# A fused attention, gated MLP and rotation kernel: batch 1's loads issued one by one, each behind a decoded tile of w_in

## The chip, the core and the metric

The program runs on one core of one Trainium2 chip. The metric is the device time in microseconds of one execution. A core has five instruction streams: PE (matmul), DVE (VectorE), ACT (ScalarE), POOL (GpSimd) and SP (SyncE, used here only to issue transfers). Each works through its own instructions in the order in which the program wrote them and waits on semaphores for the others.

## The reference

Three stages, on 4 batches of 768 tokens and 384 channels (8 heads of 48):

```python
# 1. gated linear attention, per batch and head
for t in range(S):
    state = f[:, :, t, :, None] * state + k_t (outer) v_t      # f = sigmoid(f_logit)
    y[:, :, t] = q_t @ state
# 2. gated MLP with a mixing over tokens
h = gelu_tanh(x @ w_in);  u, v = halves of h                    # w_in 384 x 1024
v_n = (v - mean(v)) / sqrt(var(v) + 1e-6) * g_ln
v_s = einsum('ts,bsd->btd', w_sg, v_n) + b_sg[None, :, None]    # w_sg 768 x 768
x = x + (u * v_s) @ w_out
# 3. rotation and a second mixing over tokens
theta = x @ w_theta
y = w_tok_r @ (x * cos(theta)) + w_tok_i @ (x * sin(theta))
u = x + y;  out = u + relu(u @ w_ch)
```

The weights arrive as 64-bit floats and are turned into 32-bit ones on the chip ("decoded").

## The kernel before

**Matmuls in three passes.** Every 32-bit operand of stages 2 and 3 is split into a high and a low part (`ACT` writes the high part, `DVE` subtracts and writes the low one), and a product is three matmuls (L782 to L784).

**Decoding.** A weight tile is loaded as raw 64-bit words into a buffer `st` (or `raw`), then one ACT instruction (L431) and four DVE instructions (L432 to L435) build the 32-bit value in `dt`, and L445 (ACT) and L446 (DVE) write its two parts to their place. `w_in` is cut into 12 tiles of 128x256, in the program's order (column block 2, k 0 to 2), (block 3, k 0 to 2), then blocks 0 and 1. Blocks 2 and 3 give v (one matmul group of 512 columns for each 128 tokens), blocks 0 and 1 give u. "Background" tiles (w_theta, w_ch and the two big mixing weights) go through the two `raw` buffers and are stored decoded to device memory for later.

**Attention.** A batch is done in two halves of 384 tokens, a half in four units of two heads. A half loads `f` (one tile, a single buffer `f` for all halves but one) and four `qkv` tiles. For batches 1 to 3 the loads are issued on POOL, for batch 0 on SP. Then, for batches 1 to 3: ACT computes the sigmoid by Tanh and Copy (L568, L569), DVE scans it (L572, L577), ACT takes Ln and Exp (L582, L583), and each unit has four products on DVE (L611 to L614), transposes (L627), state updates and scores on PE (L639, L648), a masked copy on DVE (L660), a chain of five or six small DVE steps that carry the state (L676, L680, L685, function `state`), and two more groups of matmuls (L703, L721).

**Order.** The body records operations in a `Plan`, each with an engine, a duration written by hand and a due time `vt`. A list scheduler then fixes the order of every engine's instructions, from these durations alone. `Buf` objects carry the dependencies that the scheduler sees. The semaphores that the chip waits for are put in afterwards, from the memory that the instructions really touch; an order that the scheduler chose between a POOL and an SP instruction that share no memory is therefore not enforced on the chip, while two instructions on one engine keep theirs. While PE has nothing to do in the first 100 us of the plan, the scheduler fills in matmuls of an identity (L1031), whose results nobody reads.

**The gate.** All loads of batches 1 to 3 come, in the plan, behind one POOL instruction, a copy of one element of the last decoded tile of `w_in` (L1041, k 2 of block 1) into the tile `gate`; the object that stands for it is called `first`, and the loads name it as a dependency (`later`).

Of the kernel before, what the change touches and what calls it, by code (L numbers as in the profile page):

```python
# [8 lines left out]
F32 = mybir.dt.float32  # L9
F32R = mybir.dt.float32r  # L10
I32 = mybir.dt.int32
# [6 lines left out]
P = 128  # L18
# [5 lines left out]
NK = DM // P  # L24
# [5 lines left out]
QKV = 2 * TH + NC2 * 2 * D + HP - D  # L30
WC = 256
# [28 lines left out]
HF0, HF1, V_AT, U_AT, DENSE = (-60.0, -40.0), (-25.0, -10.0), -35.0, -27.0, -33.0  # L60
# [262 lines left out]
def body(tc, ctx, att, qkv, flog, w_in, g_ln, w_sgT, b_sg, w_out, w_theta, w_rT, w_iT, w_ch, out):  # L323
    nc = tc.nc
# [19 lines left out]
        nc.vector.memset(t, value)  # L344
        return t

    gate = const.tile([P, 1], F32, name="gate")
    halfpi = fill("halfpi", math.pi / 2)
    mhalf = fill("mhalf", -0.5, NS)
    bends = const.tile([P, B, 2, NP, NC2], F32, name="bends")  # L350
# [15 lines left out]
    def make_state(attention):  # L366
# [21 lines left out]
        g.scr2 = [Buf(t=scratch2) for _ in range(2)]  # L388
        return g

    def nothing():
        pass

# [5 lines left out]
    def dma(pl, eng, nbytes, fn, r=(), w=(), wp=(), vt=None):  # L399
        pl.op(eng, {"SP": 0.47, "ACT": 0.66, "POOL": 1.05}[eng], fn, r, w, wp, dma=nbytes, vt=vt)  # L400
# [10 lines left out]
    def load_f32(pl, g, d, src, vt, background=False):  # L411

        n = src.shape[-1]
        get = lambda: d.t[:, :n]
        if src.dtype != I64:
            dma(pl, "SP", n * 512, lambda: nc.sync.dma_start(get(), src), w=[d], vt=vt - 3)
            return
        raw = pl.buf(g.raw if background else g.st, [P, 2 * TH], I32)
        dma(pl, "SP", n * 1024, lambda: nc.sync.dma_start(raw.t[:, : 2 * n], src.bitcast(I32)), [], [raw], vt=vt - 3)

        def bits():
            r = raw.t[:, : 2 * n].rearrange("p (n two) -> p n two", two=2)
            return r[:, :, 0], r[:, :, 1]

        def op(dur, fn, eng="DVE"):
            pl.op(eng, dur, fn, [raw], [d], vt=vt)

        V, iget = nc.vector, lambda: get().bitcast(I32)


        op(a1(n), lambda: nc.scalar.activation(get(), bits()[1].bitcast(F32), AF.Abs), "ACT")  # L431
        op(v2(n), lambda: V.tensor_scalar(get(), get(), TINY, None, ALU.max))  # L432
        op(v2(n), lambda: V.tensor_scalar(iget(), iget(), 3, 0x3FFFFFFF, ALU.logical_shift_left, ALU.bitwise_and))
        op(v1(n), lambda: V.scalar_tensor_tensor(iget(), bits()[1], -0x40000000, iget(), ALU.bitwise_and, ALU.bitwise_or))  # L434
        op(v1(n), lambda: V.scalar_tensor_tensor(iget(), bits()[0], 29, iget(), ALU.logical_shift_right, ALU.bitwise_or))  # L435
# [75 lines left out]
                half(pl, g, b, hf, x, carry, v0 + hf * (NP + 1) * step, step)  # L511
        return xst

    first = Buf()

    def half(pl, g, b, hf, xst, carry, vt, step):
        A = nc.scalar.activation
        eng = "SP" if b == 0 else "POOL"
# [10 lines left out]
            tiles = [(t, t) for t in (pl.buf(g.qkv, [P, QKV]) for _ in range(NP))]  # L529
        groups = (GROUPS0, GROUPS1)[hf] if b == 0 else [(0, NP)]  # L530
        qk, parts = [], []
        later = [first] if b else []
        for p, (t, root) in enumerate(tiles):
            for p0, p1 in groups:
                if p0 == p:
                    dma(
                        pl, eng, P * (p1 - p0) * TH * 4,
                        lambda gp=slice(p0, p1): q[eng].dma_start(f.t[:, gp], flog[b, hf][:, gp]), later, wp=fp[p0:p1],
                    )
            part = [Buf(of=root) for _ in range(3)]  # L540
            dma(pl, eng, P * QKV * 4, lambda t=t, p=p: q[eng].dma_start(t.t, qkv[b, p, hf]), later, wp=part)
            qk.append(t)
            parts.append(part)
        pl.vt = vt
# [43 lines left out]
    def unit(pl, g, b, hf, p, f, fb, seed, sb, be, bb, t, parts, xst, carry):  # L588
# [84 lines left out]
        def state(c):  # L673
            (s0, b0), (s1, b1) = S[c], S[c + 1]
            if hf == 0 and c == 0:
                pl.op("DVE", 0.117, lambda: V.tensor_copy(s1(), U(0)), r=[ps], w=[b1])  # L676
            elif c % 2 or c == 0:
                b1 = fulls[c // 2] if c % 2 else b1
                s1 = (lambda: st.t[:, 2 * NC2 + c // 2]) if c % 2 else s1
                pl.op("DVE", 0.117, lambda: V.tensor_add(s1(), s0(), U(c)), r=[ps, b0], w=[b1])  # L680
            else:
                be_ = be[:, c // 2 - 1 : c // 2]
                pl.op(
                    "DVE", 0.117,
                    lambda: V.scalar_tensor_tensor(s1(), st.t[:, 2 * NC2 + c // 2 - 1], be_, U(c), ALU.mult, ALU.add), r=[ps, fulls[c // 2 - 1], bb], w=[b1],  # L685
                )
            if c % 2:
                s2, b2 = S[c + 1]
                pl.op(
                    "ACT", 0.23, lambda: nc.scalar.activation(s2(), s1(), AF.Copy, scale=be[:, c // 2 : c // 2 + 1]), r=[bb, fulls[c // 2]], w=[b2]  # L690
                )
# [342 lines left out]
    with tc.manual_schedule():  # L1034
        def between():

            weights_in(pl, g, (2, 3), V_AT)
            weights_in(pl, g, (0, 1), U_AT)
            last = g.win[NK - 1][1]
            pl.op(  # L1040
                "POOL", 0.1, lambda: nc.gpsimd.tensor_copy(gate, win[:, 1, NK - 1, 2 * WC - 1 : 2 * WC].bitcast(F32)), [last], [first],  # L1041
                vt=U_AT,
            )
            pl.vt = U_AT
            dma(pl, "SP", 2048, lambda: nc.sync.dma_start(gcol, g_ln), wp=[g.const])
            dma(pl, "SP", P * 3072, lambda: nc.sync.dma_start(bbc, b_sg.partition_broadcast(P)), wp=[g.const])

        x = attention(pl, g, 0, *HF0, (*HF1, between))
        pl.vt = DENSE
# [187 lines left out]
```

## Time and profile before

| | |
|---|---|
| median of 3 runs | 677.27 us (672.85 to 678.81) |
| the profiled execution | 677.74 us, of which the trace spans 676.0 us |
| PE busy | 616.3 us, 91% of the span |
| DVE busy | 453.6 us, 67% |
| ACT busy | 342.3 us, 51% |
| POOL busy | 99.5 us, 15% |
| mean granted TensorE clock | 0.975 |

A busy share is an average over stages. The first 60 us belong to batch 0's attention and the decoding, with few real matmuls; then, to about 350 us, the first part of stage 2 and the attention of batches 1 to 3 run side by side with the background decoding; the last half is almost only matmuls. Granted clock is the clock that PE was given, as a share of 2.4 GHz: 1.00 is 2.4, 0.50 is 1.2 GHz.

### The profile page before, as it was taken

The page shows a single profiled execution, that of the slowest core. Times are in us where ns is not written, and L with a number is a line of the kernel's source. Part 1 is how long each engine was busy: PE and PEld are TensorE (multiplying, and loading weights), DVE is VectorE, ACT ScalarE, POOL GpSimd, SP SyncE. Part 2 cuts the span into 40 slices and gives each one's busy share as a digit, 9 for nine tenths or more (in the row PEclk, how much of TensorE's full clock was granted, in tenths as well). Part 3 has the DMA queues.
Part 4 walks back from the last instruction along what each step waited for, and adds up shares of the span by engine and source line. Part 5 has one row for each costly group of instructions (what it writes and reads, how often), then busy time and mean ns, then how long its engine had stood idle before and what let it go on. Part 6 is the DMA issues. An engine that isn't in the chain of part 4 may idle for free.

```text
span 676.0 us, 15027 instructions
## 1 busy us (share of the span) xinstructions
PE 616.3 (91%) x5953; PEld 569.8 (84%) x5953; DVE 453.6 (67%) x1077; ACT 342.3 (51%) x728; POOL 99.5 (15%) x178
## 2 busy tenths in 40 slices
PE   8788688989999988988989999899999999999996
PEld 8667567778788876878878999799989998998995
DVE  6999778969999897889979333741482175148203
ACT  6658587646685665675536421740291055019200
POOL 2000222143241340341131100000000000000000
PEclk9899969999999998999999999999999999999998
DMA  9522836377578787477575455058628844860762
GB/s 331 190 84 74 285 120 217 120 264 270 170 252 248 245 258 270 147 245 250 173 264 212 144 190 182 23 165 253 207 77 277 252 154 156 252 219 25 250 194 76
DMA packets 49296, 131.50 MB, mean 195 GB/s; under 512 B 6816, under 2 KB 17248, under 8 KB 48960
## 3 DMA queue, kind: packets, MB, share of 16 engines
q1 hardware_dynamic: 38656, 88.95, 41.2%
q0 software_dynamic: 10560, 41.49, 17.7%
q8 instruction: 49, 0.80, 0.5%
q14 instruction: 31, 0.25, 0.1%
HBM read 100.93 MB, written 24.77 MB: 186 GB/s over the span
## 4 chain that ended last, share of the span: by engine, by line
PE 42%; DVE 23%; ACT 11%; DMA 11%; issue 9%; POOL 2%; SPq 0%; DVEq 0%; POOLq 0%; ACTq 0%
PE mm L782 14%; PE mm L783 13%; PE mm L784 13%; DMA f<-in_flog 3%; DMA scratch<-wt 3%; DMA dt<-in_w_sgT 2%; DMA raw<-in_w_iT 2%; DVE s L680 2%; DVE dt L434 1%; DVE dt L435 1%; ACT ar L791 1%; DVE s L685 1%; DVE am L660 1%; POOL xst L755 1%; DVE tmp L845 1%
## 5 line engine op out<-in xcount | busy, mean ns | idle before, releaser
L782 PE MATMUL mm<-st,ar 128*128 128x384 f32 x480 | 164.9, 344 | 2.5 <-DMA st<-scratch 2.4
L783 PE MATMUL mm<-st,ar 128*128 128x384 f32 x480 | 161.4, 336 | 0.0
L784 PE MATMUL mm<-st,ar 128*128 128x384 f32 x480 | 161.4, 336 | 0.0
L801 ACT CAST x<-xst 128x384 fp32r<-128x384 f32 x72 | 36.9, 513 | 146.8 <-DVE xst L806 126.7
L806 DVE TENSOR_TENSOR xst<-xst,mm 128x384 f32<-128x384 f32 x48 | 25.7, 552 | 115.4 <-PE mm L784 115.4
L782 PEld LDWEIGHTS mm<-st,ar 128*128 128x128 f32 x480 | 90.9, 189 | 5.1 <-DMA st<-scratch 2.7
L783 PEld LDWEIGHTS mm<-st,ar 128*128 128x128 f32 x480 | 91.0, 190 | 0.1
L784 PEld LDWEIGHTS mm<-st,ar 128*128 128x128 f32 x480 | 90.8, 189 | 0.0
L782 PE MATMUL mm<-win,x 128*128 128x512 f32 (+1 forms) x144 | 56.6, 393 | 7.4 <-DVE tmp L845 3.7
L782 PE MATMUL mm<-x,win 128*128 128x384 f32 x168 | 58.4, 348 | 0.0
L784 PE MATMUL mm<-win,x 128*128 128x512 f32 (+1 forms) x144 | 54.1, 376 | 3.0 <-DVE x L802 3.0
L791 ACT CAST ar<-tmp 128x384 fp32r<-128x384 f32 x80 | 37.7, 509 | 37.7 <-DVE tmp L850 36.8
L784 PE MATMUL mm<-x,win 128*128 128x384 f32 x168 | 56.3, 335 | 0.0
L783 PE MATMUL mm<-x,win 128*128 128x384 f32 x168 | 56.2, 335 | 0.0
L783 PE MATMUL mm<-win,x 128*128 128x512 f32 (+1 forms) x144 | 53.5, 372 | 0.1
L802 DVE TENSOR_TENSOR x<-xst,x 128x384 fp32r<-128x384 f32 x72 | 37.8, 553 | 7.7 <-ACT x L801 6.4
L792 DVE TENSOR_TENSOR ar<-tmp,ar 128x384 fp32r<-128x384 f32 x80 | 41.0, 553 | 0.7 <-ACT ar L791 0.2
L782 PE MATMUL mm<-ar,wout 128*128 128x384 f32 x96 | 35.6, 371 | 4.2 <-DVE tmp L845 2.4
L782 PEld LDWEIGHTS mm<-win,x 128*128 128x128 f32 x144 | 27.8, 193 | 13.1 <-DVE tmp L845 5.4
L784 PE MATMUL mm<-ar,wout 128*128 128x384 f32 x96 | 33.3, 347 | 1.1 <-DVE wout L446 1.1
L755 POOL DMA_DIRECT2D xst<-y x60 | 30.7, 516 | 20.8 <-ACT y L732 10.9
L783 PE MATMUL mm<-ar,wout 128*128 128x384 f32 x96 | 33.4, 348 | 0.4 <-DVE ar L792 0.4
(146 smaller groups left out, 1227.2 us busy)
## 6 DMA issues: line engine op xcount, KB each, us to landing
st<-scratch SPq DMA_DIRECT2D x132, 384.0 KB, 3.8
qkv<-in_qkv POOLq DMA_DIRECT2D x24, 536.0 KB, 6.1
scratch<-wt POOLq DMA_DIRECT2D x24, 384.0 KB, 4.1
raw<-in_w_rT SPq DMA_DIRECT2D x12, 384.0 KB, 5.7
raw<-in_w_iT SPq DMA_DIRECT2D x12, 384.0 KB, 3.9
f<-in_flog POOLq DMA_DIRECT2D x6, 768.0 KB, 4.8
scratch<-st POOLq DMA_DIRECT2D x12, 384.0 KB, 6.7
out<-xst SPq DMA_DIRECT2D x24, 192.0 KB, 2.0
```

What stands on the lines that cost most here:

```text
L434: op(v1(n), lambda: V.scalar_tensor_tensor(iget(), bits()[1], -0x40000000, iget(), ALU.bitwise_and, ALU.bitwise_or))
L435: op(v1(n), lambda: V.scalar_tensor_tensor(iget(), bits()[0], 29, iget(), ALU.logical_shift_right, ALU.bitwise_or))
L680: pl.op("DVE", 0.117, lambda: V.tensor_add(s1(), s0(), U(c)), r=[ps, b0], w=[b1])
L755: lambda r0=r0, n=n, kc=kc, o=64 * j + off: q[yq].dma_start(xst.t[r0 : r0 + n, kc], y.t[o : o + n].rearrange("p i a t -> p (i a t)")),
L782: nc.tensor.matmul(o, h0, h1, start=start, stop=False)
L783: nc.tensor.matmul(o, h0, l1, start=False, stop=False)
L784: nc.tensor.matmul(o, l0, h1, start=False, stop=stop)
L791: pl.op("ACT", a1(n), lambda: nc.scalar.copy(tiles()[0], src.t[:, :n]), [src], [hi])
L792: pl.op("DVE", v1(n), lambda: V.tensor_sub(tiles()[1], src.t[:, :n], tiles()[0].bitcast(F32)), [src, hi], [lo])
L801: pl.op("ACT", a1(TH), lambda: nc.scalar.copy(X[hf][:, 0, k], T()), [src], [hi])
L802: pl.op("DVE", v1(TH), lambda: V.tensor_sub(X[hf][:, 1, k], T(), X[hf][:, 0, k].bitcast(F32)), [src, hi], [lo])
L806: pl.op("DVE", v1(TH), lambda: V.tensor_add(T(), T(), ps.t[:, :TH]), [ps], [xst[hf].parts[k]])
```

## The change

`gate` gets six columns and `first` becomes a list of six objects, `loaded`, one for each of the first six decoded tiles of `w_in` (blocks 2 and 3). For each of them POOL copies one element into its column. Only the loads of batch 1's first half name these: `f` the first tile, `qkv` 0 to 3 the second to the fifth. The loads of `g_ln` and `b_sg` name the first, and all background loads name the sixth. Batches 2 and 3 and the second half of batch 1 name none; their buffers hold them back. In `state` the three durations that the scheduler reckons with, 0.117 us each, become 0.2, 0.16 and 0.19.

```diff
-    gate = const.tile([P, 1], F32, name="gate")
+    gate = const.tile([P, 2 * NK], F32, name="gate")
+    loaded = [Buf() for _ in range(2 * NK)]
...
-        dma(pl, "SP", n * 1024, lambda: nc.sync.dma_start(raw.t[:, : 2 * n], src.bitcast(I32)), [], [raw], vt=vt - 3)
+        dma(pl, "SP", n * 1024, lambda: nc.sync.dma_start(raw.t[:, : 2 * n], src.bitcast(I32)), [loaded[-1]] if background else [], [raw], vt=vt - 3)
...
-    first = Buf()
...
-        later = [first] if b else []
+        gate_ = lambda i: [loaded[i]] if b == 1 and hf == 0 else []
...
-                        lambda gp=slice(p0, p1): q[eng].dma_start(f.t[:, gp], flog[b, hf][:, gp]), later, wp=fp[p0:p1],
+                        lambda gp=slice(p0, p1): q[eng].dma_start(f.t[:, gp], flog[b, hf][:, gp]), gate_(0), wp=fp[p0:p1],
...
-            dma(pl, eng, P * QKV * 4, lambda t=t, p=p: q[eng].dma_start(t.t, qkv[b, p, hf]), later, wp=part)
+            dma(pl, eng, P * QKV * 4, lambda t=t, p=p: q[eng].dma_start(t.t, qkv[b, p, hf]), gate_(p + 1), wp=part)
...
-                pl.op("DVE", 0.117, lambda: V.tensor_copy(s1(), U(0)), r=[ps], w=[b1])
+                pl.op("DVE", 0.2, lambda: V.tensor_copy(s1(), U(0)), r=[ps], w=[b1])
...
-                pl.op("DVE", 0.117, lambda: V.tensor_add(s1(), s0(), U(c)), r=[ps, b0], w=[b1])
+                pl.op("DVE", 0.16, lambda: V.tensor_add(s1(), s0(), U(c)), r=[ps, b0], w=[b1])
...
-                    "DVE", 0.117,
+                    "DVE", 0.19,
...
-            last = g.win[NK - 1][1]
-            pl.op(
-                "POOL", 0.1, lambda: nc.gpsimd.tensor_copy(gate, win[:, 1, NK - 1, 2 * WC - 1 : 2 * WC].bitcast(F32)), [last], [first],
-                vt=U_AT,
-            )
             pl.vt = U_AT
-            dma(pl, "SP", 2048, lambda: nc.sync.dma_start(gcol, g_ln), wp=[g.const])
-            dma(pl, "SP", P * 3072, lambda: nc.sync.dma_start(bbc, b_sg.partition_broadcast(P)), wp=[g.const])
+            for i, on in enumerate(loaded):
+                t, c, k = (gate[:, i : i + 1], *divmod(i, NK))
+                src = win[:, 1, k, (c + 2) * WC : (c + 2) * WC + 1].bitcast(F32)
+                pl.op("POOL", 0.1, lambda t=t, src=src: nc.gpsimd.tensor_copy(t, src), [g.win[k][c + 2]], [on], vt=U_AT)
+            dma(pl, "SP", 2048, lambda: nc.sync.dma_start(gcol, g_ln), [loaded[0]], wp=[g.const])
+            dma(pl, "SP", P * 3072, lambda: nc.sync.dma_start(bbc, b_sg.partition_broadcast(P)), [loaded[0]], wp=[g.const])
```

After the change every line number from about L395 on is 1 to 3 higher. Since a list scheduler sets the order, every engine's order changes from the first microseconds on. Two places matter most.

POOL, from the second seed fill of batch 0 (`ar2`) on, before. `f0`, `qkv0` to `qkv3` are batch 1's first half, `gate` the gate, `stat0` the statistics of v:

```order
L551 MEMSET ar2_0_114 128x384 x4
L567 MEMSET seed0_415 128x1536
L981 TENSOR_TENSOR stat0_865<-stat0_865,mhalf_81 128x3
L1041 COPY gate_78<-win_87 128x1
L538 DMA f0_1089<-in_flog 128x1536
L541 DMA qkv0_1102<-in_qkv 128x1072
L541 DMA qkv1_1116<-in_qkv 128x1072
L541 DMA qkv2_1130<-in_qkv 128x1072
L541 DMA qkv3_1143<-in_qkv 128x1072
L490 DMA scratch1_91<-st2_1091 128x768
```

The same place of POOL, after:

```order
L553 MEMSET ar2_0_115 128x384 x4
L569 MEMSET seed0_409 128x1536
L1045 COPY gate_78<-win_87 128x1
L540 DMA f0_523<-in_flog 128x1536
L1045 COPY gate_78<-win_87 128x1 x2
L543 DMA qkv0_842<-in_qkv 128x1072
L1045 COPY gate_78<-win_87 128x1
L543 DMA qkv1_860<-in_qkv 128x1072
L1045 COPY gate_78<-win_87 128x1
L543 DMA qkv2_882<-in_qkv 128x1072
L1045 COPY gate_78<-win_87 128x1
L543 DMA qkv3_900<-in_qkv 128x1072
```

The five loads moved from behind the first statistics of v to ahead of them, each behind its copy, in POOL's own order.

DVE, from the split of the last tiles of `w_in` (`st2` to `st4` are the first tiles of w_sg) to batch 1's first scan (L577 on `f0`), before:

```order
L446 TENSOR_TENSOR win_87<-dt2_1048,win_87 128x256
L993 SCALAR_TENSOR_TENSOR ar0_0_997<-tmp1_895,stat0_865,ar0_0_997 128x512
L993 SCALAR_TENSOR_TENSOR ar0_0_997<-tmp2_911,stat0_865,ar0_0_997 128x512
L742 TENSOR_TENSOR y1_1038<-y1_1038,at1_100 48x3x64 x2
L802 TENSOR_TENSOR x1_90<-xst1_0_726,x1_90 128x384
L446 TENSOR_TENSOR st2_1091<-dt0_1054,st2_1091 128x384
L446 TENSOR_TENSOR st3_1097<-dt1_1061,st3_1097 128x384
L446 TENSOR_TENSOR st4_1122<-dt2_1087,st4_1122 128x384
L572 TENSOR_SCALAR seed0_415<-f0_1089 128x12
L577 SCALAR_TENSOR_TENSOR f0_1089<-f0_1089,seed0_415 128x1536
L614 TENSOR_TENSOR qkv0_1102<-qkv0_1102,f0_1089 128x384
L802 TENSOR_TENSOR x1_90<-xst1_0_726,x1_90 128x384
```

DVE around the same scan (now L579) after the change:

```order
L437 SCALAR_TENSOR_TENSOR dt0_519<-st3_182,dt0_519 128x256
L601 TENSOR_TENSOR ar2_0_115<-ar2_0_115 128x384
L436 TENSOR_SCALAR dt1_367<-dt1_367 128x256
L436 TENSOR_SCALAR dt2_373<-dt2_373 128x256
L574 TENSOR_SCALAR seed0_409<-f0_523 128x12
L437 SCALAR_TENSOR_TENSOR dt1_367<-st1_173,dt1_367 128x256
L437 SCALAR_TENSOR_TENSOR dt2_373<-st2_178,dt2_373 128x256
L438 SCALAR_TENSOR_TENSOR dt0_519<-st3_182,dt0_519 128x256
L579 SCALAR_TENSOR_TENSOR f0_523<-f0_523,seed0_409 128x1536
L603 SCALAR_TENSOR_TENSOR ar1_0_146<-ar2_0_115,ar1_0_146 128x384
L438 SCALAR_TENSOR_TENSOR dt1_367<-st1_173,dt1_367 128x256
L438 SCALAR_TENSOR_TENSOR dt2_373<-st2_178,dt2_373 128x256
```

The scan moved from behind all 12 tiles of `w_in` and three tiles of w_sg into the decoding of the first five tiles, among the last products of batch 0's attention.

## Rows read from the trace of the kernel before

**Rows 1.** Busy time by stretch: PE, PEld, DVE, ACT, POOL, granted clock, DMA share, GB/s

```profile
204.00:250.00 46.00, 43.40 (x600) 39.97 (x601) 43.43 (x102) 30.42 (x57) 15.20 (x27) 1.00 0.76 242
450.00:500.00 50.00, 49.56 (x290) 48.81 (x289) 19.55 (x40) 15.16 (x32) 0.00 (x0) 1.00 0.71 221
```

**Rows 2.** The same view in stretches of 4 us

```profile
76.00:80.00 4.00, 1.21 (x8) 0.89 (x6) 0.96 (x2) 3.45 (x3) 0.00 (x0) 1.00 1.04 382
80.00:84.00 4.00, 0.95 (x3) 0.52 (x4) 3.97 (x4) 0.82 (x2) 0.00 (x0) 0.73 1.03 350
84.00:88.00 4.00, 3.05 (x7) 1.86 (x6) 1.98 (x5) 3.94 (x4) 1.07 (x2) 0.50 0.81 326
88.00:92.00 4.00, 1.66 (x6) 1.66 (x7) 3.31 (x7) 3.88 (x9) 0.00 (x0) 0.50 0.25 98
```

**Rows 3.** Chain of work that ended last: start us, us, what

```profile
74.30 9.37 DMA dt<-in_w_sgT
...
84.22 1.28 ACT L311
```

**Rows 4.** DVE in order of time: start us, us, line, idle before and its releaser

```profile
79.00 0.18 DVE L572 TENSOR_SCALAR seed<-f 128x12 f32<-128x12 f32 x1 [4.69 <-ACT f L569]
79.22 3.36 DVE L577 TENSOR_TENSOR_SCAN f<-f,seed 128x1536 f32<-128x1536 f32 x1
...
88.55 0.56 DVE L611 TENSOR_TENSOR qkv<-qkv,seed 128x384 f32<-128x384 f32 x1 [2.57 <-ACT seed L583]
...
94.72 0.21 DVE L676 COPY s<-at 128x48 f32<-128x48 f32 x1 [0.55 <-PE at L648]
...
107.09 0.18 DVE L572 TENSOR_SCALAR seed<-f 128x12 f32<-128x12 f32 x1 [1.71 <-ACT f L569]
...
150.55 0.18 DVE L572 TENSOR_SCALAR seed<-f 128x12 f32<-128x12 f32 x1 [4.98 <-ACT f L569]
```

**Rows 5.** POOL in order of time

```profile
70.41 0.64 POOL L1041 COPY gate<-win 128x1 f32<-128x1 f32 x1 [7.02 <-DVE win L446]
71.00 0.73 POOL L538 DMA_DIRECT2D f<-in_flog  x1
71.73 2.09 POOL L541 DMA_DIRECT2D qkv<-in_qkv  x4
```

**Rows 6.** ACT in order of time

```profile
75.97 1.49 ACT L568 ACTIVATE f<-f 128x1536 f32<-128x1536 f32 x1 [2.73 <-DMA f<-in_flog]
77.49 1.48 ACT L569 ACTIVATE f<-f 128x1536 f32<-128x1536 f32 x1
...
83.69 0.51 ACT L445 CAST st<-dt 128x384 fp32r<-128x384 f32 x1 [2.06 <-DMA dt<-in_w_sgT]
```

**Rows 7.** DVE groups, 0 to 130 us: busy us, mean ns, idle before

```profile
L660 DVE TENSOR_TENSOR am<-at,mask 128x384 f32<-128x384 f32 x13 | 7.2, 551 | 0.0
L680 DVE TENSOR_TENSOR s<-s,at 128x48 f32<-128x48 f32 x34 | 6.9, 202 | 0.9
L434 DVE SCALAR_TENSOR_TENSOR dt<-st,dt 128x256 int32<-128x256 int32 x12 | 4.8, 420 | 0.0
L561 DVE TENSOR_TENSOR_SCAN ar<-ar 128x384 f32<-128x384 f32 x4 | 3.8, 954 | 0.1
```

**Rows 8.** From issue to landing of batch 1's first `qkv` loads (60 to 80 us)

```profile
DMA to landing us min/median/max: 6.4/8.5/11.0
```

**Rows 9.** PE in order of time, two matmuls and its next wait

```profile
84.28 0.63 PE L782 MATMUL mm<-win,x 128*128 128x512 f32 x1
84.71 0.63 PE L783 MATMUL mm<-win,x 128*128 128x512 f32 x1
...
90.34 0.90 PE L627 MATMUL at<-ident,qkv 128*128 128x128 f32 x3 [3.30 <-DVE qkv L613]
```

**Rows 10.** Who waited for whom: PE for the state chain, whole span

```profile
PE at L703 <- DVE s L680: 11.9, 11, 2.0
PE at L703 <- DVE s L685: 6.9, 8, 1.6
```

## The prediction

> **What bounds the kernel now.** I read the busy time by stretch first. In the second half of the span PE is busy 49.56 of 50 us [rows 1]: nothing but matmuls, and the change touches nothing there. From about 100 to 350 us PE and DVE are both nearly full (43.40 and 43.43 of 46 us [rows 1]). So what an edit near the start wins or loses is handed on to the end as a shift, if neither engine gets new work or new waits. Nor does either: instructions are moved, and six tiny ones are added on POOL.
>
> Finer stretches then show the hole that the change is about. From 76 to 92 us PE is busy 1.21 + 0.95 + 3.05 + 1.66 = 6.9 of 16 us, part of it at 0.50 of its clock, while the DMA engines are full until 84 us [rows 2]. The POOL rows say why: the gate waits for the last tile of w_in, opens at 70.41, and all five loads of batch 1 go out within 3 us [rows 5]. They are 2.9 MB with 0.58 MB of w_sg beside them. The chain has a w_sg load of 9.37 us there [rows 3], the `qkv` loads land in 6.4 to 11.0 us [rows 8], and `f` holds up ACT until 75.97 [rows 6]. DVE, which had been full, then sits 4.69 us in front of the scan, 2.57 in front of the first product, 0.55 for PE and 1.71 in front of the second scan [rows 4]: 9.5 us between 74 and 107 us. PE's waits (3.30 us for a product of DVE [rows 9]) are the shadow of these. **DVE is the engine to count**, since it bounds all of the start.
>
> **The change, part by part.**
>
> *The five loads move.* After, POOL has the first copy and `f` behind the first decoded tile, and a copy ahead of each `qkv` load. On DVE the first tile is done some 40 us before the last one was. Does `f` then arrive in time for the scan, which also moved forward? Between the first tile's split and the scan's seed the new DVE order has, by my count, 16 state steps, 3 masked copies, 2 scans of 384, 7 products, 5 small bend steps and final adds, and 7 decode steps. At 0.20, 0.55, 0.95, 0.55, some 0.2 to 0.3 and 0.3 to 0.4 us [rows 7], the products being of the size of L660, that is about 14 us, some 13 with the overlap of neighbours. The load's own chain is 0.64 (copy) + 4.97 (issue at 71.00 to Tanh at 75.97) + 1.49 + 1.48 [rows 5, 6] = 8.6 us, about 10.5 with a table load of 1.28 [rows 3] and a 384-wide ACT step between. It is covered; at the slowest landing of a load beside it, 11.0 us [rows 8], it would be late by 3 us. So the 4.69 us go. For `qkv` 0 the copies ahead of it follow the second and third tile to finish, near 54 us by the count on DVE; with 6.4 us [rows 8] it lands near 61, as DVE comes to it. I take 0, with an upper end of 11.0 - 6.4 = 4.6. Ln and Exp lie beside the decoding, so the 2.57 us go too.
>
> *w_sg loads no longer meet batch 1's loads*, which takes the 9.37 us out of the chain. What is next in line there is DVE itself, and that is in the sum already.
>
> *What the DVE gets in return.* Scan (3.36 us [rows 4]) and products now stand ahead of most of w_in, so the statistics of v come some 3 us and the u tiles some 5 us later than before. That by itself costs nothing at the end: up to the first residual of p4 the two DVE orders hold the same instructions (both reach it as entry 316 of the order), so DVE gets there earlier by the waits removed less the waits that come. New waits: (a) the second scan of batch 1 still waits for its `f`, which can be loaded only when the first half has let go of the single buffer; 1.71 us before [rows 4], and I put 1.7 to 2.9 (the price of Tanh and Copy, 2.97 [rows 6]); (b) v of the second three token blocks now waits for the splits of x, which stand behind more on DVE, and PE may come to it cold: 27 matmuls at a step of 0.43 us [rows 9] in place of half of that at full clock are 5.8 us if all are cold, nothing if none; I put 0 to 2.5; (c) POOL's power and ACT's scaling of v in front of DVE, 0 to 1 us, from the 0.55 wait [rows 4] below and the 1.71 above. Sum: -9.5 + (1.7 to 2.9) + (0 to 2.5) + (0 to 1) = -7.8 to -3.1. I take the middle, **-5.5 us**.
>
> *Three tables swapped earlier.* ACT now changes from Ln/Exp to Tanh and back within batch 0's last units, and the two changes around 84 us go: the order has six table loads up to the first residual both before and after, at 1.28 us each [rows 3]. By the rows this is 0. The Trainium skill, ScalarE: Activation LUTs, section "Table sets: the hidden batching unit", speaks against the move: it says to batch calls by table set, since a switch costs the load and a drain, 2.66 us in all. No row here shows the drain; by the page's price two switches in a stretch where ACT is nearly full would give back up to 2.7 us of the sum (about 675).
>
> *Six POOL copies.* 0.64 us each [rows 5], on an engine that waited 7.02 us there and much longer before; they stand ahead of the first statistics, but those need all six tiles anyway. 0, at most 0.64 if the sixth comes last.
>
> *Background, g_ln and b_sg.* They are issued on SP, and the copies run on POOL; the kernel's own waits come from memory that is touched, so they wait only by their place in SP's queue, behind the stores of attention. Two loads of 0.4 MB move from 20 to about 58 us, into DMA time that is little used. 0 either way, within the 0.55 us that DVE waits for a neighbour [rows 4].
>
> *The three durations.* A state step takes 0.20 us and more [rows 7], the plan reckoned with 0.117. With 0.16 to 0.2 the scheduler puts PE's next group (L703) later. PE waited 11.9 + 6.9 = 18.8 us for such steps [rows 10], but by my count half of it in the first 64 us, where few real matmuls wait. Between a gain of some 6 us (a third of the 18.8) and a loss of the same size, since every order behind changes, I take 0.
>
> The profiled execution took 677.74 us, 0.5 above the median; 677.74 - 5.5 = 672.2, say **672 us**.
>
> **The rivals.**
>
> *The gain is swallowed (677).* The next scan of that kind, batch 2's, waits 4.98 us at 150 us for its own `f` [rows 4], and that load too comes behind a single buffer, stores and w_sg. If DVE comes to it 5.5 us earlier and the load does not, the wait grows to 10.5 us and all is as it was. For it: the buffer, and the queue of POOL stores. Against it: the load is issued when a DVE product lets the buffer go, and that product comes earlier as well.
>
> *More than the start (666).* If PE and DVE agree better with the new durations, a third of the 18.8 us [rows 10] goes too: 672 - 6.3 = 665.7.
>
> *Slower, PE cold through the whole of the start (684 to 688).* The work that DVE now does first leaves PE with two holes, before batch 1's first transposes and before the splits of x's second half. If the clock drops at the first and stays at 0.50 until w_sg's matmuls run, as it did from 84 to 92 us [rows 2], then 36 u matmuls, 27 for v and half of w_sg's 72 run at steps that are 0.15 to 0.21 us longer: 36 x 0.15 + 27 x 0.21 + 36 x 0.15 = 16.5 us (the 384-wide ones taken as three quarters of 0.21). Less the 5.5, that is +11, or 688; with a third of it hidden behind DVE, 683. It decides if the granted clock is under 0.75 on the mean from 64 to 100 us. For it: PE was at 0.50 after some 6 us with little work [rows 2]. Against it: DVE, not PE, sets the pace there, and the plan has fill matmuls in both holes. On this the Trainium skill, TensorE: Matmul & The Clock Gate, section "HAM oscillation — how this bites in real kernels", says that waits between bursts of matmuls let the clock fall and that the next burst starts slow; the row at 84 us agrees with 0.50.
>
> *It does not do what it says.* For the background loads this is so, as told, and changes nothing; for batch 1's loads POOL's order enforces it.
>
> **How the numbers follow.** Forecast (-3 to -8): 0.47. Swallowed: 0.25. More: 0.12. Cold and slower: 0.16. One per cent, 6.8 us, is about what a measurement of this kernel can tell from no change: its three runs lie 0.9% apart. Faster by over 1% (under 670.5) is the third of the forecast next to its lower end and the "more" case, and a little of the others: 0.36. Slower by over 1% (over 684) is most of the cold case and accidents of the new order: 0.16. The rest, 0.48, is within 1%. The range takes in the "more" case and the near end of the cold one: 662 to 683; the forecast's own is 669 to 675.
>
> **What would show it.** Right: the `f` load issued near 32 us, `qkv` near 55 to 60; no wait over 1 us in front of the first scan; w_sg loads near 4 us; the first tmp<-mm of batch 0 (L845, 113.9 us before) 5 to 8 us earlier; the matmul-only half starting some 5 us earlier. Wrong: a DVE wait over 3 us for `f` or `qkv` 0, or ACT so full from 36 to 56 us that DVE waits for its casts; a granted clock near 0.5 from 64 to 100 us; or the start earlier as told and the lead gone by 160 us.

## The result and the profile after

The kernel after takes 680.39 us (median of 17, 677.14 to 684.45), the kernel before 676.52 (17 runs beside it). The ratio is 1.0061, interval 1.0042 to 1.0080: about 4 us slower, where 5.5 us faster was predicted. The profiled execution took 679.54 us (span 677.8). A ratio leaves disturbed executions out, so here and below it need not be the quotient of the medians beside it.

Line numbers after are 1 to 4 higher than before. The first place is the start. POOL of the kernel after, the time from the issue of `f` to its landing, and ACT:

```profile
30.24 0.18 POOL L1045 COPY gate<-win 128x1 f32<-128x1 f32 x1 [4.89 <-DVE win L449]
30.36 0.73 POOL L540 DMA_DIRECT2D f<-in_flog  x1
```

```profile
DMA to landing us min/median/max: 9.8/9.8/9.8
```

```profile
35.80 1.28 ACT L311 ACT_TABLE_LOAD   x1
40.21 1.48 ACT L570 ACTIVATE f<-f 128x1536 f32<-128x1536 f32 x1 [3.12 <-DMA f<-in_flog]
```

`f` is issued 41 us earlier than before [rows 5], but lands after 9.8 us; ACT waits 3.12 us for it, and what is queued behind Tanh waits too. DVE of the kernel after:

```profile
43.19 0.20 DVE L682 TENSOR_TENSOR s<-carry,at 128x48 f32<-128x48 f32 x1 [2.62 <-PE at L650]
...
45.93 0.17 DVE L574 TENSOR_SCALAR seed<-f 128x12 f32<-128x12 f32 x1
...
97.79 2.08 DVE L995 SCALAR_TENSOR_TENSOR ar<-tmp,stat,ar 128x512 fp32r<-128x512 f32 x3 [1.54 <-ACT ar L991]
...
101.98 0.21 DVE L678 COPY s<-at 128x48 f32<-128x48 f32 x1 [1.64 <-PE at L650]
...
106.02 0.18 DVE L574 TENSOR_SCALAR seed<-f 128x12 f32<-128x12 f32 x1 [2.75 <-ACT f L571]
106.23 3.36 DVE L579 TENSOR_TENSOR_SCAN f<-f,seed 128x1536 f32<-128x1536 f32 x1
```

Compare with [rows 4]. The first scan's seed no longer waits (45.93), nor does the first product (no wait stands on DVE between 53.1 and 95 us). But four waits are new or longer: 2.62, 1.54, 1.64 and 2.75 us. The second scan comes at 106.23 instead of 107.30, and the first residual at 136.92 instead of 134.95.

The second place is one that the prediction did not look at: 300 to 312 us, batch 3's last scan. DVE and PE of the kernel after:

```profile
303.92 0.18 DVE L574 TENSOR_SCALAR seed<-f 128x12 f32<-128x12 f32 x1 [3.21 <-ACT f L571]
304.13 3.36 DVE L579 TENSOR_TENSOR_SCAN f<-f,seed 128x1536 f32<-128x1536 f32 x1
307.41 0.53 DVE L449 TENSOR_TENSOR wt<-dt,wt 128x384 fp32r<-128x384 f32 x1
307.86 1.02 DVE L616 TENSOR_TENSOR qkv<-qkv,f 128x384 f32<-128x384 f32 x2
310.83 0.25 DVE L1097 TENSOR_REDUCE low<-bends 128x1 f32<-128x96 f32 x1 [1.96 <-ACT bends L583]
311.00 2.18 DVE L847 SCALAR_TENSOR_TENSOR tmp<-mm,gcol,bbc 128x384 f32<-128x384 f32 x4
```

```profile
311.67 0.44 PE L784 MATMUL mm<-x,win 128*128 128x384 f32 x1 [2.76 <-DVE tmp L847]
```

`low` is the minimum over all bends, which chooses between the fast path and the general one. Its line stands behind the planned part of the program, and no table of the plan gives it a place. It waits 1.96 us for the last bends, and the four products that PE needs stand right behind it. In the kernel before, the same stretch of DVE reads:

```profile
303.38 0.18 DVE L572 TENSOR_SCALAR seed<-f 128x12 f32<-128x12 f32 x1 [1.82 <-ACT f L569]
...
308.26 0.36 DVE L432 TENSOR_SCALAR dt<-dt 128x384 f32<-128x384 f32 x1
...
311.06 0.25 DVE L1096 TENSOR_REDUCE low<-bends 128x1 f32<-128x96 f32 x1
311.22 0.61 DVE L845 SCALAR_TENSOR_TENSOR tmp<-mm,gcol,bbc 128x384 f32<-128x384 f32 x1
```

There decode steps lie between the scan and `low`, the bends are ready in time, and nothing waits. The busy time from batch 1's last residual to batch 2's first, after and then before (length, PE, PEld, DVE, ACT, POOL, granted clock, DMA share, GB/s):

```profile
279.13:339.43 60.30, 54.73 (x706) 49.20 (x708) 52.81 (x130) 36.17 (x78) 16.54 (x30) 0.97 0.65 214
```

```profile
279.39:337.53 58.14, 53.95 (x710) 47.67 (x708) 53.46 (x130) 36.72 (x78) 16.48 (x29) 1.00 0.69 225
```

As many DVE instructions, 130, take 2.2 us longer. PE's wait is not the whole of it: behind it the granted clock falls. PE in two stretches of 4 us, from the same view:

```profile
308.00:312.00 4.00, 1.24 (x8) 0.92 (x7) 2.04 (x5) 3.21 (x4) 0.57 (x1) 1.00 0.95 343
312.00:316.00 4.00, 4.00 (x17) 4.00 (x16) 3.90 (x9) 2.28 (x3) 0.00 (x0) 0.61 0.04 15
```

After 2.76 us without a matmul PE runs some 1 us at the full clock and then at 1.2 GHz: from 312.82 to 316.28 its matmuls follow each other in 0.32 us instead of 0.17, 11 steps, so by an estimate from these rows 1.6 us on top of the wait. In the kernel before the clock is 1.00 in the whole stretch.

### The profile page after: what moved, and what is told of

The parts are those of the page before. It is cut to its first block, busy times and chain, and to the rows that moved or that the text cites. A ratio compares the mean times of both kernels' runs of the same rounds, so it can differ in the third digit from the quotient of the medians.

```text
span 677.8 us, 15200 instructions
## 1 busy us (share of the span) xinstructions
PE 622.1 (92%) x6029; PEld 578.0 (85%) x6029; DVE 454.7 (67%) x1077; ACT 341.4 (50%) x728; POOL 100.5 (15%) x183
## 4 chain that ended last, share of the span: by engine, by line
PE 53%; DVE 18%; DMA 11%; ACT 9%; issue 7%; POOL 2%; SPq 0%; DVEq 0%; POOLq 0%; ACTq 0%
PE mm L784 16%; PE mm L785 16%; PE mm L786 16%; DMA xst<-y 3%; DMA f<-in_flog 3%; DMA scratch<-wt 2%; DVE dt L438 1%; DMA st<-in_w_in 1%; ACT ar L793 1%; DVE s L682 1%; DMA raw<-in_w_rT 1%; DVE dt L437 1%; DVE dt L436 1%; DVE s L687 1%; PE mm L1033 1%
## 5 line engine op out<-in xcount | busy, mean ns | idle before, releaser
L784 PE MATMUL mm<-x,win 128*128 128x384 f32 x168 | 59.4, 354 | 3.8 <-DVE tmp L847 3.8
L784 PE MATMUL mm<-win,x 128*128 128x512 f32 (+1 forms) x144 | 56.2, 391 | 3.9 <-DVE tmp L847 3.1
L786 PE MATMUL mm<-x,win 128*128 128x384 f32 x168 | 57.6, 343 | 0.0
L785 PE MATMUL mm<-x,win 128*128 128x384 f32 x168 | 57.5, 342 | 0.0
L785 PE MATMUL mm<-win,x 128*128 128x512 f32 (+1 forms) x144 | 53.0, 368 | 0.1
L786 PE MATMUL mm<-win,x 128*128 128x512 f32 (+1 forms) x144 | 52.8, 367 | 0.0
L784 PEld LDWEIGHTS mm<-x,win 128*128 128x128 f32 x168 | 32.5, 193 | 5.2 <-DVE tmp L847 4.3
L784 PE MATMUL mm<-ar,wout 128*128 128x384 f32 x96 | 35.0, 365 | 1.8 <-DVE tmp L899 1.8
L1033 PE MATMUL mm<-ident 128*128 128x128 f32 x252 | 34.6, 294 | 1.6 <-POOL ident masks.py:199 1.6
```

What stands on the lines that cost most here:

```text
L784: nc.tensor.matmul(o, h0, h1, start=start, stop=False)
L785: nc.tensor.matmul(o, h0, l1, start=False, stop=False)
L786: nc.tensor.matmul(o, l0, h1, start=False, stop=stop)
L1033: nc.tensor.matmul(g.mm.tiles[i][:, :P], ident, ident, start=True, stop=True)
```

## The experiments

Three ideas stood at first. *A*: the early loads spoil the start. *B*: the new durations make the worse order. *C*: any other order is worth half a per cent either way. All of the table's ratios are against the kernel before, run beside it.

| run | what it is | median us | ratio (95%) | first residual at | 279 to 339 us takes |
|---|---|---|---|---|---|
| after | | 680.39 | 1.0061 (1.0042 to 1.0080) | 136.9 | 60.3 |
| e1 | durations alone | 677.05 | 1.0047 (1.0016 to 1.0079) | 134.0 | 60.2 |
| e2 | gates alone | 672.97 | 0.9961 (0.9926 to 0.9997) | 129.9 | 59.8 |
| e3 | start after, rest before | 674.27 | 0.9988 (0.9952 to 1.0024) | 133.9 | 56.5 |
| e4 | start before, rest after | 682.56 | 1.0119 (1.0075 to 1.0164) | 137.2 | 61.8 |
| e5 | after to 236 us, then before | 675.86 | 0.9986 (0.9963 to 1.0010) | 135.8 | 56.6 |
| e6 | before to 236 us, then after | 686.43 | 1.0147 (1.0107 to 1.0186) | 137.4 | 62.2 |
| e7 | before, batch 3's `f` later | 683.50 | 1.0093 (1.0058 to 1.0128) | 139.3 | 56.4 |
| e8 | after, g_ln and b_sg later | 680.25 | 1.0060 (1.0036 to 1.0085) | 134.2 | 61.8 |
| e9 | after, `low` later | 677.07 | 0.9982 (0.9952 to 1.0012) | 133.3 | 57.2 |
| e10 | start of e2, rest before | 668.50 | 0.9873 (0.9834 to 0.9913) | 129.5 | 57.5 |
| e11 | e2, g_ln and b_sg later | 673.32 | 0.9921 (0.9888 to 0.9954) | 130.4 | 60.4 |
| e12 | before, WAIT2 0.07 | 676.86 | 0.9987 (0.9957 to 1.0016) | 136.7 | 58.6 |
| e13 | e8 and e9 together | 676.15 | 1.0006 (0.9979 to 1.0032) | 134.9 | 57.2 |
| e14 | before, `low` later | 677.93 | 1.0004 (0.9966 to 1.0042) | 140.1 | 57.3 |
| e15 | e4, `low` later | 681.23 | 1.0078 (1.0043 to 1.0112) | 136.7 | 58.7 |
| e16 | e10, g_ln and b_sg later | 670.46 | 0.9928 (0.9891 to 0.9966) | 128.9 | 57.4 |

The last two columns are from each run's one profile: the start of the first `xst<-xst,mm` on DVE, and the way from the twelfth to the thirteenth of them (e2 and e11 have a third order there, with 764 and 765 PE instructions instead of 698 to 711, so these two do not compare).

**e1 and e2: the two halves of the change.**

```diff
-                pl.op("DVE", 0.117, lambda: V.tensor_add(s1(), s0(), U(c)), r=[ps, b0], w=[b1])
+                pl.op("DVE", 0.16, lambda: V.tensor_add(s1(), s0(), U(c)), r=[ps, b0], w=[b1])
```

e1 has this and its two neighbours alone, e2 everything else.

> The kernel before with the three new state durations and nothing else; the loads of batch 1 stay behind the last tile. Before is 676.5, after 680.4. Theory A (the start is spoiled by the early loads themselves: f lands late, ACT, PE and DVE wait for it, and the first residual comes 2 us later; durations do nothing): 676 to 677.5. Theory B (the new durations make the worse order, the loads alone would gain): 679 to 682. Theory C (any change of the plan's numbers shuffles the order and moves the time by some 0.5% either way): anywhere in 673 to 682, and the place where it wins or loses lies behind the first residual.

> The kernel after with the old state durations of 0.117: all loads let go as in the change, but the plan reckons as before. Theory A (the start is spoiled by the early loads): 679 to 681, like after. Theory B (the durations cost): 670 to 676, the gain of the start comes out at the end. Theory C (order shuffle): anywhere in 673 to 682.

e1 is slower, e2 faster, and the two intervals do not meet. A falls with e2, which has the early loads and is faster than the kernel before. The signs are B's, but e1 loses less than B said: its median of 677.05 lies in the range of A, not in that of B, and C's wide range takes in e1 and all but takes in e2. Beside the gates the durations cost 1.0061 - 0.9961 = 1.0%, 6.8 us.

**e3 and e4: start and rest apart.** One kernel makes both orders and joins them: one order up to a residual, then whatever is left, in the other order.

```diff
+        (head, at), (tail, at2) = self.under(HEAD), self.under(TAIL)
+        cut = [i for i, (o, _) in enumerate(head) if not isinstance(o, tuple) and (o.kw or {}).get("mark") == CUT]
+        cut = cut[0] + 1 if cut else len(head)
+        done = {o for o, _ in head[:cut] if not isinstance(o, tuple)}
...
-        for o, load in self.schedule():
+        for o, load in self.mixed():
```

> Two plans in one kernel: up to the first residual of batch 0 every engine has the order of the kernel after, and what is left has the order of the kernel before. Theory A (the start costs): like after, 679 to 681, with the first residual near 137. Theory B or C (the start is no worse, the order behind it costs): 675 to 677, like before. If the start were faster and the rest ate it: under 675.

> The other half: up to the first residual the order of the kernel before, then the order of the kernel after. Theory A: like before, 676 to 677.5. Theory B or C: like after, 679 to 682. If both halves cost, each of the two mixed kernels shows some 2 us over before.

The rest costs: 1.2% behind the old start (e4 against before), 0.7% behind the new one (after against e3). The new start is worth 0.1% (e3 against before, an interval that takes in 1) to 0.6% (after against e4).

**e5, e6 and e7: where in the rest.** e5 and e6 have the seam at the ninth residual, near 236 us. e7 moves one transfer of the kernel before on POOL, batch 3's first `f` load, to behind the store of the next residual:

```diff
+MOVES = [(1483, 1000)]
```

> Two plans in one kernel again, with the seam later: every engine has the order of the kernel after up to the last of batch 1's three first-half residuals (236 us), what is left has the order of the kernel before. It tells where behind the first residual the new order loses. Theory L (the loss is made before 236 us: batch 3's f is asked for 5 us later, since the products that let go of its buffer stand behind state steps): 679 to 682, with a PE wait of some 7 us near 258. Theory M (the loss is made behind 236 us: Ln of batch 3 behind a decode step that waits for its load, transposes ahead of the v matmuls): 674 to 677 and no PE wait over 4 us.

> The other half of the same cut: the order of the kernel before up to that residual, then the order of the kernel after. Theory L: 675 to 677.5, since f is asked for as early as before. Theory M: 680 to 683 with a PE wait of 7 us or more near 258.

> The kernel before with one instruction moved: batch 3's first f load stands on POOL behind the next residual's store, some 5 us later (where the kernel after has it); all other orders are as before. Theory L: the scan of batch 3 comes some 5 us later, PE waits 6 us or more near 255, and the time is 679 to 682. Theory M: the scan comes later, but the time stays within 2 us of before (675 to 678).

The seam says M: e5 is as fast as before, e6 as slow as e4 or slower. What is lost lies behind 236 us. But M's mark was wrong: e6, at 686.43 us above M's range, has no PE wait over 4.61 us from 236 to 279 us. The longest PE waits of that stretch in e5 and in the kernel after are these:

```profile
247.77 0.92 PE L779 MATMUL at<-am,qkv 64*64 64x64 f32 x24 [9.10 <-DVE s L760]
```

```profile
258.50 0.88 PE L629 MATMUL at<-ident,qkv 128*128 128x128 f32 x3 [7.92 <-issue]
```

e5 loses nothing by its wait; the kernel after, with 7.92 us, even covers the stretch from 232 to 279 us faster than the kernel before (46.8 against 47.9 us). The longest wait of a trace was no loss; other waits of the same stretch had gone for it. The stretch that differs is the next one, the last column of the table. e7, at 683.50 us, came out above both ranges. DVE in front of batch 3's first scan, in e7 and in the kernel before:

```profile
246.39 0.18 DVE L651 TENSOR_SCALAR seed<-f 128x12 f32<-128x12 f32 x1 [5.92 <-ACT f L648]
```

```profile
236.39 0.27 DVE L572 TENSOR_SCALAR seed<-f 128x12 f32<-128x12 f32 x1 [1.22 <-ACT f L569]
```

Where the transfer is late and the order stays, DVE waits 5.92 us instead of 1.22, and the kernel loses 0.9%. So L names a real price, only not the one that the change paid: e5, which has the transfer where the change has it, is not slower than before.

**e8: why `f` is late in the start.**

```diff
-            dma(pl, "SP", 2048, lambda: nc.sync.dma_start(gcol, g_ln), [loaded[0]], wp=[g.const])
-            dma(pl, "SP", P * 3072, lambda: nc.sync.dma_start(bbc, b_sg.partition_broadcast(P)), [loaded[0]], wp=[g.const])
+            dma(pl, "SP", 2048, lambda: nc.sync.dma_start(gcol, g_ln), [loaded[-1]], wp=[g.const])
+            dma(pl, "SP", P * 3072, lambda: nc.sync.dma_start(bbc, b_sg.partition_broadcast(P)), [loaded[-1]], wp=[g.const])
```

> The kernel after with g_ln and b_sg let go by the sixth tile instead of the first. On SP the two loads move 12 places back; PE, DVE, ACT and POOL have the same order as after. If the broadcast b_sg load is what made f land 9.8 us after its issue, f lands in 5 to 6 us, ACT's wait for it (3.1 us) and DVE's 2.6 us at 43 us go, and the first residual comes 2 to 3 us earlier; the time is 677 to 679 if that is handed on to the end and 680 if not. If f is late for another reason: f still takes 9 to 10 us and the time is 680.

The load's path to landing and ACT in e8:

```profile
DMA to landing us min/median/max: 5.5/5.5/5.5
```

```profile
35.07 1.28 ACT L311 ACT_TABLE_LOAD   x1
36.37 1.49 ACT L570 ACTIVATE f<-f 128x1536 f32<-128x1536 f32 x1
```

5.5 us instead of 9.8 (and 5.5 again in e13, which has the same two loads moved), no wait on ACT, and DVE's 2.62 us at 43 us are gone. The first residual came 2.7 us earlier than in the profile of after, the time did not move. In the other kernels with the order of after the load was quicker also without this: it landed after 8.1 (e3), 7.8 (e5) and 7.2 us (e9). The 9.8 us of the one profile were a slow case.

**e9 and e14: one instruction.** `low` moves behind batch 2's first residual, where the bends have long been written; in e14 the same in the kernel before.

```diff
+            def add():
+                V.tensor_add(T(), T(), ps.t[:, :TH])
+                if late:
+                    V.tensor_reduce(low, bends.rearrange("p b h n c -> p (b h n c)"), mybir.AxisListType.X, ALU.min)
...
-    nc.vector.tensor_reduce(low, bends.rearrange("p b h n c -> p (b h n c)"), mybir.AxisListType.X, ALU.min)
```

> The kernel after with one DVE instruction moved: the minimum over the bends (low, 0.25 us), which no plan places and which stands right behind batch 3's last scan, waits there 1.96 us for ACT in front of the four tmp products that PE waits for (2.76 us at 311). It now stands behind batch 2's first residual; everything else is in the order of after. If this wait is what the new order loses between 279 and 339 us (60.3 against 56.5 to 58.1 us): PE's wait at 311 shrinks to under 1 us, the stretch to about 58, and the time is 676 to 678.5. If the loss is spread over the order: PE waits elsewhere and the time is 680 to 681.

> The control: the kernel before with low moved in the same way. There low does not wait and no product that PE waits for stands behind it. If its wait is what counts: 675.5 to 677.5, no change. If moving it helps by itself: 672 to 674.

DVE of e9 at the place (L857 is L847 there), PE, and the busy time of the stretch:

```profile
304.88 1.02 DVE L616 TENSOR_TENSOR qkv<-qkv,f 128x384 f32<-128x384 f32 x2
305.82 2.18 DVE L857 SCALAR_TENSOR_TENSOR tmp<-mm,gcol,bbc 128x384 f32<-128x384 f32 x4
```

```profile
306.49 0.44 PE L787 MATMUL mm<-x,win 128*128 128x384 f32 x1
```

```profile
276.49:333.65 57.16, 53.55 (x707) 47.69 (x709) 52.45 (x129) 35.95 (x78) 16.53 (x30) 1.00 0.68 225
```

The four products follow the scan at once, PE has no wait in front of `mm<-x,win`, the clock stays at 1.00, and 3.1 us of the stretch are gone. The time falls from 1.0061 to 0.9982. In the kernel before, where `low` waits for nothing, moving it does nothing (1.0004). The other traces agree: in all five kernels that have the new rest, or in e1 the new durations, with `low` in its place (after, e1, e4, e6, e8) `low` waits 1.9 to 2.9 us, PE waits 2.6 to 3.6 us in front of `mm<-x,win`, and the clock of the stretch is 0.94 to 0.97; in the kernels with the old rest neither waits and the clock is 1.00.

**e13 and e15: is that all?** Both are joined from edits shown above.

> The kernel after with both small moves: low behind batch 2's first residual, g_ln and b_sg behind the sixth tile. With the two loads moved alone (e8) the first residual came 2.7 us earlier in the profile and the time did not move, since low's wait stood in the way behind it. If that is so, the lead now reaches the end: 672 to 675.5. If the lead is lost elsewhere: 676.5 to 678, as e9.

> e4 (start of before, rest of after; 1.2% slower) with low moved. If low's wait and what hangs on it is the whole loss of the new rest: 676 to 678. If it is a part: 679 to 681. If the new rest costs for other reasons: 682 as e4.

Behind the new start it is: e9, with the new rest, is as fast as e3, with the old one (0.9982 and 0.9988). Behind the old start it is not. e15 is 0.8% slower than before, clear of 1; by the middles of two intervals that overlap it is 0.4% faster than e4, so some two thirds of the new rest's loss are still there. e13 is no faster than e9; its profile has the first residual at 134.9, no earlier than e9's 133.3, so it does not tell whether a lead would have been handed on.

**e10, e11 and e16: the lead handed on.** e10 joins the start that the gates make with the old durations to the rest of the kernel before.

> Up to the first residual the order that the gates make with the old durations (it came there 5 us before the kernel before), then the order of the kernel before. If a lead is handed on to the end, as the prediction took it, when the order behind is left alone: 670 to 673. If the rest swallows it (batch 2's scan waits longer for its f): 675 to 677.

> The kernel after with the old durations and with g_ln and b_sg behind the sixth tile: against e2_gates only two loads on SP have moved. f then does not share the DMA engines with the broadcast: if that is worth anything at the end, 670 to 672; if not, as e2_gates, 672 to 675.

> e10 (start by the gates with the old durations, rest of before; 1.3% faster) with g_ln and b_sg behind the sixth tile. In that start nothing waits for f, so the two loads are in nobody's way: 667 to 670, as e10. If they cost there too: 664 to 666.

e10 beats both kernels: 668.50 us, 0.9873 of before, better than was expected of a lead that is handed on. DVE of e10 at the second scan, the only wait above 1.7 us between 20 and 140 us:

```profile
100.09 0.18 DVE L647 TENSOR_SCALAR seed<-f 128x12 f32<-128x12 f32 x1 [4.99 <-ACT f L644]
```

Moving g_ln and b_sg helps neither clearly: e11's interval overlaps that of e2, e16's that of e10.

**e12: how much is another order worth?**

```diff
-WAIT2 = 0.065
+WAIT2 = 0.07
```

> The kernel before with one number of the plan moved a little: WAIT2 from 0.065 to 0.07, which changes 76 lines of DVE's order and 56 of PE's and nothing of what the kernel does. A measure of what a reordering by itself is worth: if it moves the time by less than 0.2% (675.5 to 678), a difference of 0.6% or more between two orders needs a place and a cause; if by 0.5% or more, orders are a lottery at that size and the new durations need no special reason to cost what they cost.

0.9987, and 1 lies inside the interval. This is one reordering, smaller than that of the change, and no proof that all are harmless; but it gives C no support.

## Why the prediction was wrong

**The step that failed: "Between a gain of some 6 us (a third of the 18.8) and a loss of the same size, since every order behind changes, I take 0."** The three durations are the part of the change that decided. Beside the gates they cost 6.8 us (after against e2), by themselves 0.5% or 3.2 us (e1). The bound was right in size; the middle was taken where neither end had been looked at. The gain that the prediction had in mind is there: PE's waits for the state chain, 18.8 us before [rows 10], come to 9.2 + 5.4 = 14.6 us in the kernel after:

```profile
PE at L705 <- DVE s L682: 9.2, 8, 2.5
PE at L705 <- DVE s L687: 5.4, 5, 2.4
```

In e1 they are 13.3 us; with the old durations behind the gates they are 18.5 in e2 and 15.2 in e11. The new order loses more elsewhere, in two places. In the start, the gates with the old durations bring the first residual to 128.9 to 130.4 us (e2, e10, e11, e16); with the new ones it comes at 133.3 to 136.9 (after, e3, e5, e8, e9, e13). (Without the gates it is not so: e1 reaches it at 134.0, no later than the kernel before, in its one profile.) 1.1 us of DVE's time there are a centring step that takes 1.62 instead of 0.49 us in these six kernels and in no other (last section). Behind the start, the new order takes 60.2 to 62.2 us from 279 to 339 us (after, e1, e4, e6, e8) where the old rest takes 56.4 to 58.1 (before, e3, e5, e7, e10, e14, e16). Most of this difference is `low` and what stands behind it: 57.2 to 58.7 with it out of the way (e9, e13, e15). Its price is made of PE's wait and of the half clock behind that wait.

**"A shift, if neither engine gets new work or new waits. Nor does either"** was half wrong. The shift itself is handed on: in e10 the start is 8.1 us earlier than the mean of the six profiles with the old start (137.6; before, e4, e6, e7, e14, e15), and the end 1.27% or 8.6 us. So with the old durations the gates give about what their sum of -7.8 to -3.1 us said: against the one profile that the prediction read (134.95) the lead is 5.4 us. Luck has a part in that, since not all terms are as put: in e10 (a), the second scan's wait, is 4.99 us and (c) 1.68, with (b) at nothing. But the change did bring new waits far behind the place of its edits, through the order.

**The five loads.** Issued at 30.4, 56.4, 57.1, 58.0 and 59.8 us, as worked out (32, 55 to 60). The waits of 4.69 and 2.57 us went as told, and `qkv` 0 made none. The transfers of w_sg got as quick as told: the six from 60 to 110 us land in 2.3 to 4.9 us, median 2.7 (before 2.3 to 10.8, median 5.5), and ACT waits 1.1 us for them in all instead of 4.5. `f` was "covered" by a margin of 3 us that one slow landing (9.8 us) used up; e8 shows that the cover holds at 5.5 us.

**The new waits** were put at 1.7 to 6.4 us together. Between 95 us and the first residual DVE's idle time is 8.0 us after and 6.2 to 9.1 in the four kernels with that start; it was 1.7 in the profile of before, but 3.7 to 5.8 in the other five with the old start, so the profile that the prediction read was a lucky one. (a) The second scan is as told, 2.75. (c) Scaling v, "0 to 1", took 1.54. (b) Cold v matmuls did not come: the granted clock is 1.00 from 60 to 95 us, as this row of after shows beside [rows 2]; it is 0.88 only behind that.

```profile
60.00:95.00 35.00, 32.78 (x442) 28.69 (x442) 33.92 (x99) 22.88 (x61) 4.06 (x6) 1.00 0.45 145
95.00:137.00 42.00, 35.09 (x482) 30.58 (x480) 33.27 (x79) 27.48 (x53) 10.93 (x20) 0.88 0.54 180
```

Not on the list were waits for PE's scores (1.64 at 101.98, 0.90 at 115.17, 0.98 at 122.50). So with the new durations the start gained 2.6 us on the mean (137.6 against 135.0 in after, e3, e5 and e9), not 5.5; in the profile of after the first tmp<-mm of batch 0 comes at 111.61, 2.3 us earlier and not 5 to 8.

**Table loads.** There are six up to the first residual before and after, as counted. e2 has eight there and is the faster one. The next activation follows a load at once (35.07 + 1.28 and Tanh at 36.37 in e8), so the drain that the Trainium skill, ScalarE: Activation LUTs, section "What ACT_TABLE_LOAD costs", adds to a load shows in no row here; the estimate of 675 that went by it was no better than the sum.

**POOL copies, background, g_ln and b_sg at 0.** The copies took 0.18 us where one shows alone. g_ln and b_sg cost nothing that the end shows (e8), though b_sg can delay `f`. Background loads were not tried alone.

**The rivals.** *Swallowed* by batch 2's scan: no; in e10, with a lead of 8 us, its wait is 2.07 us instead of 4.98, and 3.32 in the kernel after. *Cold PE*: no, the clock is 1.00 from 64 to 100 us, where it was 0.81 before. Neither saw that an unplanned instruction may take the place of a wait.

**What stays open.** About 0.8% of the new rest behind the old start (e15). Its rows show longer waits at several places (3.52 us in front of the last scan's seed against 1.82 before, 4.31 us for ACT's half of an x split at 357), none of which was tried alone. A second hole goes with the new rest, `low` moved or not: in the 4 us up to batch 2's first residual PE is busy 0.5 to 1.7 us in the eight kernels with it (e1 counted in) and 3.5 us in the seven with the old rest, and in the 4 us behind it the clock is 0.50 to 0.70 there and 1.00 here. But e9 has this hole too and is not slower than before, so by itself it does not tell where the 0.8% lie. Why longer, truer durations lead the scheduler to these orders was not tried either.

## What to carry to other kernels

Where a list scheduler sets the order, a number in its table is a change to the whole program: time it apart from the edit that it comes with, since here loads that gained and durations that lost made one change that looked like nothing but a small loss. An instruction that the plan does not know (here a reduction of 0.25 us) can cost ten times its length when its wait falls in front of work that another engine waits for (here TensorE, which came back from the wait to half its clock), so give it a place. And a start's lead read from one profile is worth little: the same order reached the first residual anywhere from 134.9 to 140.1 us.

## What the hardware showed unexpectedly

The landing of one 0.79 MB load took 5.5 to 9.8 us in one and the same place of the order, the slowest with a broadcast of 0.39 MB issued 0.2 us ahead on another engine's queue (b_sg on SP at 30.16, `f` on POOL at 30.36), the quickest, twice, with it moved away (e8, e13). The Trainium skill, DMA: Bandwidth & Descriptors, section "Issuing engines are not separate DMA queues", says that transfers from all engines run on the same 16 DMA engines and interleave; e8 agrees, and the executions in between (7.2 to 8.1 us with the broadcast in its place) show that the order alone does not fix the time.

A centring step of 0.49 us took 1.62 us while POOL filled the next seed. DVE and POOL of the kernel after:

```profile
91.59 1.62 DVE L966 TENSOR_SCALAR tmp<-tmp,stat 128x512 f32<-128x512 f32 x1
...
93.31 0.49 DVE L966 TENSOR_SCALAR tmp<-tmp,stat 128x512 f32<-128x512 f32 x1
```

```profile
91.55 1.38 POOL L569 MEMSET seed<- 128x1536 f32 x1 [1.04 <-DVE stat L965]
```

The two began within 0.04 us of each other. The 18 profiles hold 432 such steps; 426 take at most 0.51 us, and the six others, one in each kernel with the start of after (after, e3, e5, e8, e9, e13), take 1.62 us and begin 0.03 to 0.04 us behind such a fill. In the kernel before a fill lies beside a decode step, which takes 0.36 us elsewhere (308.65); DVE and POOL there:

```profile
294.59 1.81 DVE L433 TENSOR_SCALAR dt<-dt 128x384 int32<-128x384 int32 x1
```

```profile
294.78 1.40 POOL L567 MEMSET seed<- 128x1536 f32 x1
```

Additions and products with two inputs keep their 0.55 us beside a fill (at 137.53 and 138.00 in the kernel before). No run moved a fill by itself, so the cause rests on this pairing.
